# A block-convolution and token-mixer kernel: a second fold of the kv transform, Nyquist rows on column tiles, and a rewritten instruction order

## The chip, the core and the metric

The kernel runs on one core of a Trainium2 chip. The core has five engines with separate instruction streams: TensorE (PE; its weight loads are listed as PEld), VectorE (DVE), ScalarE (ACT), GpSimd (POOL) and SyncE (SP, which issues DMAs only; so can POOL). Each engine takes its instructions strictly in the order of its stream and waits on semaphores for the others. The metric is the device time of one execution in microseconds (us).

## What is computed

Two branches share the input x = A_q and are mixed by a gate. With S = 2048, D = 640, F = 1536:

```python
k_shift = sum over t of 4:  k_pad[:, t:t+S, :] * shift_k[:, 3 - t]
kv  = k_shift * v
kv_f = rfft(kv padded to 4096);  kf_f = rfft(ssm_k padded to 4096)
y   = irfft(kv_f * kf_f)[:S] + kv * ssm_D
a   = q * y
h   = layernorm(q)                       # over D
b   = (gelu(h^T @ w1 + b1) @ w2 + b2)^T  # mixes the tokens
g   = sigmoid((q * gate_w).sum(-1))
out = g * a + (1 - g) * b
```

## The kernel before

**The convolution.** The 2048 positions are cut into P = 4 blocks of n = 512. Filter block i (`W0` to `W3`) and kv block j (`A0` to `A3`) are taken to the frequencies of a length of 1024 by matmuls with cosine and sine tables (`TFc`, `TFs` for the filter, `AFc`, `AFs` for kv, `TI` for the way back). The frequencies stand in four groups `fi` of 128: groups 0 and 1 hold the odd ones, 2 and 3 the even ones. Before its transform a block is folded: its second half is added to and subtracted from the first half in reverse order, so that a matmul contracts 256 positions (two sub-blocks of 128) instead of 512. For the filter the folded tile is `en`, which is then transposed to `eo`; for kv it is `es`. Output block m sums over j <= m the products of `A_j` with the combined filter `W_{m-j}`; the sums are collected in `Z0`/`Z1`, and the way back (`inverse`) and `epilogue` turn `Z` into two halves `pb`, `qb` and these into rows of the output.

Per kv block (`kv_load`, `kv_block`, `a_freq`): a DMA transpose loads k as `kT`; 80 small matmuls with diagonal weights `dg` make the shifted k; ScalarE evicts it to `ks`; two DMA transposes bring it to `kn`; VectorE multiplies it by `vn` in place and folds it to `es`. `kT`, `vn` and `es` have two buffers each, `kn` and `ks` one. In `a_freq` each of 8 results (4 groups, cosine and sine) takes two sub-blocks times two halves of D, four 128x320 matmuls, and one eviction to `A`.

The **Nyquist row** (frequency 512, an alternating sum) of each filter block rides in row 0 of a sine result: in `w_freq`, four matmuls with one column of weights (`nyq`) are put between the sine matmuls of group 3, and `w_nyq` moves row 0 of `W[:, 8]` to `W[0, 4]` by one DMA of 1.2 KB behind a 160 KB copy within `W`, and clears the old row.

**The token mixer.** `bn_stats` and a scale on VectorE give `h`; 384 matmuls `h,w` with w1 (in six sets of two buffers' worth, three buffers `w1_0` to `w1_2`) give `gT`; 384 matmuls `gT,w` with w2 (buffers `w2_0`, `w2_1`) give the tiles `o1_0` to `o1_7`, each evicted with the gate factor 1 - g. Most of `o` is written out by SP, and the convolution's part is added to it in DRAM by accumulating DMAs that POOL issues (`acc0`, `acc1`); for the last block half of it is added on VectorE and written once. The gate g, the same rows reversed (`ggr`), is made by a matmul with a flip matrix from three bf16 pieces `gs`, split off on POOL in five steps (`gs`, `gd`).

**The order.** Nothing is scheduled on the chip: every operation of the program is recorded with a number, and the tuple `ORDER` lists all of them in the order in which they are emitted, found offline by a search over a cost model. Each engine's stream, and so each queue of DMAs, follows from it. A wait is emitted in the stream of the engine that issues the operation, so on SP and POOL it holds back every later DMA of that queue. PSUM has four slots of two banks, handed out in this order.

Helpers record each kind of work in one line, which is the one that the profile names: L307 matmuls, L641 `tensor_tensor`, L648/L649 `tensor_scalar`, L656 copies, L659 memsets, L683 activations, L275 plain DMAs, L262 DMA transposes, L268 indirect loads, L266/L270 accumulating stores, L864/L866 the layernorm statistics. Instructions are therefore told apart by their tiles.

Of the kernel before, what the change touches and what calls it, by code (L numbers as in the profile page):

```python
# [8 lines left out]
BF16 = mybir.dt.bfloat16  # L9
F32 = mybir.dt.float32  # L10
I32 = mybir.dt.int32
ACT = mybir.ActivationFunctionType
# [5 lines left out]
class _Tracker:  # L18
# [34 lines left out]
    def regions(self, ap):  # L53
# [4 lines left out]
        if info[0] == "DR":  # L58
            lo = hi = ap.offset
            for st, ct in ap.ap:  # L60
                lo += min(0, st * (ct - 1))
                hi += max(0, st * (ct - 1))
            return [("DR", 0, 1, lo // info[1], hi // info[1] + 1)]
# [42 lines left out]
        else:  # L106
# [10 lines left out]
            res.append((space, p0, p1, base + lo * esize, base + hi * esize))  # L117
        return res
# [197 lines left out]
def bass_gated_mix__ssm_conv_h3__mixer_token_mlp__prompt_kernel(  # L316
# [42 lines left out]
)  # L359


# [891 lines left out]
```

## Time and profile before

| | us |
|---|---|
| three runs | 203.32, 207.01, 214.42 |
| their median | 207.01 |
| the profiled execution | 202.34 |
| its span, first to last instruction | 200.5 |
| TensorE busy | 183.1 |
| VectorE busy | 179.8 |
| ScalarE busy | 119.5 |
| GpSimd busy | 89.4 |

The profile is of one execution. Its page gives the busy time of each engine, the same in 40 slices of the span, the chain of work that ended last, and groups of equal instructions with their mean duration, the idle time of the engine just before them and what ended it. Further views list the instructions of one engine in order of time (start, length, what, and the idle time before), the busy time of all engines in chosen stretches, and the DMAs with the time from issue to landing. Lengths of neighbours on TensorE and VectorE overlap a little, since they are pipelined, so the cost of one of many is the distance between starts.

### The profile page before, as it was taken

The numbers are of one execution on the slowest core, as the hardware profiler recorded it, in microseconds if no ns is written. First come the engines' busy times: TensorE is split into PE (matmuls) and PEld (weight loads), VectorE is DVE, ScalarE is ACT, GpSimd is POOL, SyncE is SP. The second block draws the span as 40 slices with busy tenths as digits, with TensorE's granted clock in tenths as the row PEclk, the third lists the DMA queues.
The fourth block names the chain that finished last, engine by engine and source line by source line (L and its number), as shares of the span: only waits on it lengthen the run. The fifth ranks groups of instructions, "written<-read, shape, count | busy, mean of one in ns | idle before, by whom it ended". The sixth has DMA issues, their size and how long they took to land.

```text
span 200.5 us, 3786 instructions
## 1 busy us (share of the span) xinstructions
PE 183.1 (91%) x1528; PEld 123.2 (61%) x1528; DVE 179.8 (90%) x227; ACT 119.5 (60%) x187; POOL 89.4 (45%) x110
## 2 busy tenths in 40 slices
PE   0599799999999999999999999849999999999991
PEld 0445363467567777667777776526776677777670
DVE  4378999788799999999999999989999799999865
ACT  5777787888995895634701478334363814551571
POOL 4320256741803564005329133963881548517560
PEclk9999999999999999999999999978999999999999
DMA  5999989999789999999659102032779868898895
GB/s 143 237 234 283 254 230 207 248 254 281 216 189 204 181 131 158 179 288 221 201 157 210 29 0 65 0 109 85 217 150 280 238 152 263 171 201 252 174 148 113
DMA packets 49731, 36.86 MB, mean 184 GB/s; under 512 B 33202, under 2 KB 46386, under 8 KB 49714
## 3 DMA queue, kind: packets, MB, share of 16 engines
q1 hardware_dynamic: 43874, 20.17, 47.6%
q0 software_dynamic: 5840, 16.45, 33.3%
q8 instruction: 12, 0.20, 0.4%
q14 instruction: 5, 0.04, 0.1%
HBM read 23.25 MB, written 4.92 MB: 140 GB/s over the span
## 4 chain that ended last, share of the span: by engine, by line
PE 50%; DMA 12%; DVE 11%; SPq 11%; POOL 9%; issue 5%; ACT 0%; DVEq 0%; POOLq 0%
PE pp L307 50%; SPq L262 7%; DVE stats L864 4%; POOL out_dram L266 4%; DMA w<-in_B_w_dram 4%; SPq L275 3%; DMA wnat<-in_A_ssm_k_dram 3%; DMA out_dram<-cg 3%; POOL gd L641 2%; DVE en L641 2%; DVE cg L641 1%; DMA out_dram<-o 1%; DMA vn<-in_A_v_dram 1%; POOL gs L656 1%; POOL xe L268 1%
## 5 line engine op out<-in xcount | busy, mean ns | idle before, releaser
L307 PE MATMUL pp<-h,w 128*128 128x320 bf16 x384 | 54.3, 299 | 0.1
L307 PE MATMUL pp<-gT,w 128*128 128x320 bf16 x384 | 53.8, 301 | 0.5 <-DMA w<-in_B_w_dram 0.5
L641 DVE TENSOR_TENSOR tT<-A,W 128x640 bf16<-128x640 bf16 (+4 forms) x44 | 48.5, 1124 | 0.7
L641 DVE TENSOR_TENSOR Z<-Z,tT 128x2560 bf16<-128x2560 bf16 (+3 forms) x35 | 47.6, 1373 | 0.6
L307 PEld LDWEIGHTS pp<-gT,w 128*128 128x128 bf16 x384 | 37.6, 99 | 15.9 <-DMA w<-in_B_w_dram 0.8
L307 PEld LDWEIGHTS pp<-h,w 128*128 128x128 bf16 x384 | 37.2, 98 | 15.3 <-issue 1.0
L275 POOL DMA_DIRECT2D w<-in_B_w_dram x18 | 18.4, 1023 | 37.2 <-PE pp L307 34.0
L683 ACT ACTIVATE o<-pp,c,omg 128x640 bf16<-128x640 f32 x16 | 14.1, 880 | 20.4 <-PE pp L307 20.4
L683 ACT ACTIVATE A<-pp 128x640 bf16<-128x640 f32 x32 | 21.3, 707 | 6.2 <-PE pp L307 6.1
L683 ACT ACTIVATE gT<-pp,bf 128x640 bf16<-128x640 f32 x12 | 9.6, 797 | 18.9 <-PE pp L307 18.9
L307 PE MATMUL pp<-Z,TI 128*128 128x320 bf16 x128 | 20.1, 310 | 0.0
L268 POOL DMA_INDIRECT xe<-in_A_q_dram,bidx x8 | 11.4, 1427 | 14.2 <-PE pp L307 7.7
L266 POOL DMA_INDIRECT out_dram<-cg,bidx x8 | 15.9, 1984 | 4.2 <-issue 1.8
L683 ACT ACTIVATE W<-pp 128x640 bf16<-128x640 f32 x24 | 15.5, 711 | 3.2 <-PE pp L307 3.0
L307 PEld LDWEIGHTS pp<-Z,TI 128*128 128x128 bf16 x128 | 12.5, 100 | 5.7 <-issue 0.4
L864 DVE BATCH_NORM_STATS2 stats<-xs 128x6 f32<-128x320 bf16 x32 | 13.8, 475 | 1.4 <-DMA xs<-in_A_q_dram 1.4
L307 PE MATMUL pp<-eo,TFs 128*128 128x320 bf16 x64 | 12.8, 323 | 1.3 <-DMA eo<-en 1.0
L683 ACT ACTIVATE ks<-pp 128x1024 bf16<-128x1024 f32 (+1 forms) x12 | 10.2, 878 | 4.2 <-PE pp L307 3.4
L307 PE MATMUL pp<-eo,TFc 128*128 128x320 bf16 x64 | 12.4, 306 | 0.0
L268 POOL DMA_INDIRECT vn<-in_A_v_dram,bidx x8 | 11.1, 1386 | 2.1 <-issue 2.1
L683 ACT ACTIVATE xs<-xs 128x640 bf16<-128x640 bf16 x16 | 11.8, 747 | 0.0
L641 DVE TENSOR_TENSOR Z<-A,W 128x5120 bf16<-128x5120 bf16 x4 | 11.3, 2817 | 0.0
(85 smaller groups left out, 227.1 us busy)
## 6 DMA issues: line engine op xcount, KB each, us to landing
w<-in_B_w_dram POOLq DMA_DIRECT2D x8, 768.0 KB, 7.3
w<-in_B_w_dram POOLq DMA_DIRECT2D x10, 512.0 KB, 5.3
wnat<-in_A_ssm_k_dram SPq DMA_DIRECT2D x4, 640.0 KB, 5.7
xs<-in_A_q_dram SPq DMA_DIRECT2D x7, 320.0 KB, 3.7
out_dram<-o SPq DMA_DIRECT2D x6, 320.0 KB, 3.6
vn<-in_A_v_dram SPq DMA_DIRECT2D x4, 320.0 KB, 7.7
xe<-in_A_q_dram SPq DMA_DIRECT2D x4, 320.0 KB, 4.4
w<-in_B_w_dram SPq DMA_DIRECT2D x4, 256.0 KB, 5.2
```

Of the source, the lines that this page charges most:

```text
L262: ins = engobj.dma_start_transpose(out_ap, in_ap)
L266: ins = engobj.indirect_dma_start(whole, off, in_ap, None, compute_op=ALU.add)
L268: ins = engobj.indirect_dma_start(out_ap, None, whole, off)
L275: ins = engobj.dma_start(out_ap, in_ap)
L307: ins = self.nc.tensor.matmul(ps_ap, lhsT=lhsT, rhs=rhs, start=start, stop=stop)
L641: return vop(eng, c, lambda e: e.tensor_tensor(out_, in0, in1, op), [in0, in1], [out_], pr)
L656: return vop(eng, c, lambda e: e.tensor_copy(out_, in_), [in_], [out_], pr)
L683: return e.activation(out_, src, func, **kw)
L864: vop("DVE", 0.41, (lambda o_, i_: lambda e: e.bn_stats(o_, i_))(o_, i_), [i_], [o_], pr)
```

## The change

1. **kv's even frequencies are folded a second time.** The sub-blocks of a kv block are now taken 256 apart (`rows2`, strides of 256 rows; tables at 512 half steps), so that the two folded sub-blocks differ, at an even frequency, only by a sign. Two VectorE instructions per block add and subtract them into a new tile `fs` (one buffer), and each even group needs one sub-block instead of two. The epilogue takes its rows in the same new grouping.
2. **Nyquist rows on four column tiles.** `nyq` becomes 32 columns wide; eight matmuls of 32 columns by 160 (two sub-blocks, four tiles) and four with a one-row operand come after the sine matmuls of group 3, and write to a part of the same PSUM bank; ScalarE evicts them to `nr`, VectorE adds neighbouring blocks' `nr`, and four small DMAs per block, instead of one, bring them to `W[0, 4]`.
3. **Gate pieces**: the five steps of `gs`/`gd` move from POOL to VectorE.
4. **w1**: the eight later loads move from POOL's queue to SP's.
5. The first filter block is loaded and folded in two parts; `cg` has four buffers instead of two, used in turn, and the accumulating stores have two semaphores each; the last block adds `o1_6` and `o1_7`'s first rows on VectorE and stores the others early.
6. `ORDER` is new throughout. The tracker of dependencies holds output rows and PSUM banks apart differently.

```diff
-        iota(b["hcol_i"][:, :], [[256, 2]], 1, 2, 0.2)
+        iota(b["hcol_i"][:, :], [[512, 2]], 1, 2, 0.2)
...
-                        f"{nm}_{t0}" if s_ < 1 else f"{nm}_p", pr + 0.35 * (8 * hf + t0), stream="SP" if s_ < 1 else "POOL")
+                        f"{nm}_{t0}" if s_ < 1 else f"{nm}_p", pr + 0.35 * (8 * hf + t0), stream="SP")
...
-                    if c == 1 and fi == 3:
-                        pairs = pairs[:1] + [(b["nyq"][:, nb:nb + 1], eo[:, 0, nb, :]) for nb in range(2)] + pairs[1:]
-                    pe([p_], halves(p_, pairs), pr)
+                    mms = halves(p_, pairs)
+                    if c == 1 and fi == 3:
+                        for nb in range(2):
+                            for g in range(4):
+                                mms.append((p_, 320, 160, b["nyq"][:, nb, :], eo[:, 0, nb, 160 * g:160 * g + 160], nb == 0, False,
+                                            32 * g))
+                        for g in range(4):
+                            mms.append((p_, 320, 160, b["onr"][:, 0:32], eo[0:1, 1, 0, 160 * g:160 * g + 160], False, True, 32 * g))
+                    pe([p_], mms, pr)
...
+                    if c == 1 and fi == 3:
+                        act(b[f"nr{i}"][:, :], (lambda p_: lambda: pp[p_.slot][:, 320:480])(p_), ACT.Copy, 1, scale=1.0 / N2, ps=[p_])
...
+            tt(b[f"nr{i}"][:, :], b[f"nr{i}"][:, :], b[f"nr{i - 1}"][:, :], ALU.add, pr)
...
-            dma(W[0:1, 4, :], W[0:1, 8, :], f"wn{i}", 17)
-            memset(W[0:1, 8, :], 0.0, 2)
+            for g in range(4):
+                dma(W[0:1, 4, 160 * g:160 * g + 160], b[f"nr{i}"][32 * g:32 * g + 1, :], f"wn{i}", 17)
...
-            dma(b[nm][:, 0, :, :], rows(A_v, 2 * i), nm, pr + 0.3)
+            dma(b[nm][:, 0, :, :], rows2(A_v, 4 * i), nm, pr + 0.3)
...
+            e2 = es_[:, :, :].rearrange("p (e k) d -> p e k d", k=2)
+            for s_, op in ((0, ALU.add), (1, ALU.subtract)):
+                tt(b[f"fs{i % NFS}"][:, s_, :, :], e2[:, :, 0, :], e2[:, :, 1, :], op, pr - 2)
...
-                    e0 = 0 if (fi >= 2) == (c == 0) else 2
-                    pairs = [(tf(tab, nb, fi), es_[:, e0 + nb, :]) for nb in range(2)]
+                    if fi >= 2:
+                        pairs = [(tf(tab, 0, fi), b[f"fs{j % NFS}"][:, 3 - fi, c, :])]
+                    else:
+                        pairs = [(tf(tab, nb, fi), es_[:, 2 - 2 * c + nb, :]) for nb in range(2)]
...
-            cgs = [b[f"cg{k}"] for k in range(2)]
+            cgs = [b[f"cg{2 * (m_ % 2) + k}"] for k in range(2)]
...
-        copy(gs[:, 0, :], gg, 20, "POOL")
-        tt(gd[:, 0, :], gg, gs[:, 0, :], ALU.subtract, 20, eng="POOL")
-        copy(gs[:, 1, :], gd[:, 0, :], 20, "POOL")
-        tt(gd[:, 1, :], gd[:, 0, :], gs[:, 1, :], ALU.subtract, 20, eng="POOL")
-        copy(gs[:, 2, :], gd[:, 1, :], 20, "POOL")
+        copy(gs[:, 0, :], gg, 20, "DVE")
+        tt(gd[:, 0, :], gg, gs[:, 0, :], ALU.subtract, 20)
+        copy(gs[:, 1, :], gd[:, 0, :], 20, "DVE")
+        tt(gd[:, 1, :], gd[:, 0, :], gs[:, 1, :], ALU.subtract, 20)
+        copy(gs[:, 2, :], gd[:, 1, :], 20, "DVE")
```

What the new order does around these edits, read off the two programs: before the first `kn` multiplication VectorE now has all eight gate multiplications (`xs,gwb`) and three of the six instructions that combine neighbouring filter blocks, where it had six and one. On SP, the load of the first `kT` moves from the eighth place to behind the second filter transpose. Between the transposes that bring in the second `kn` and the load of the third `kT`, SP has 28 DMAs where it had 8: three of the w1 loads, four copies within `W`, the 16 small DMAs of the Nyquist rows, two table transposes, one load of v, and those transposes themselves. The flip matmul of the gate comes behind 120 of the 384 `gT,w` matmuls, before behind 24. After the last `Z` TensorE has 24 `gT,w` matmuls left, before 48.

More of the change, by code (lines that the diff above doesn't have):

```diff
@@ L58, in regions @@
         if info[0] == "DR":
[L59 to L63, printed above, removed]
+            parts = [(st, ct) for st, ct in ap.ap if st > info[1]]
+            offs = [ap.offset]
+            for st, ct in parts:
+                offs = [o + st * k for o in offs for k in range(ct)]
+            ext = sum(st * (ct - 1) for st, ct in ap.ap if st <= info[1])
+            return [("DR", 0, 1, o // info[1], (o + ext) // info[1] + 1) for o in offs]
         space, base, rowsize, esize = info
@@ L117, in regions @@
             res.append((space, p0, p1, base + lo * esize, base + hi * esize))
+        if space == "PS":
+            res = [(space, p0, p1, lo // 2048 * 2048, -(-hi // 2048) * 2048) for space, p0, p1, lo, hi in res]
         return res
@@ L544, in _build @@
         buf("idp", [128, 128], BF16, 0, 34)
-        buf("nyq", [128, 2], BF16, 0, 40)
+        buf("nyq", [128, 2, 32], BF16, 0, 40)
+        for i in range(P):
+            buf(f"nr{i}", [128, 160], BF16, 8, 50)
         buf("onr", [1, 256], BF16, 0, 40)
@@ L581, in _build @@
             buf(f"es{i}", [128, NB, D], BF16, 48, 90)
-        buf("tT", [128, 8, D], BF16, 42, END)
+        NFS = 1
+        for i in range(NFS):
+            buf(f"fs{i}", [128, 2, 2, D], BF16, 48, 90)
+        buf("tT", [128, 8, D], BF16, 50, END)
         for j in range(P):
@@ L788, in _build @@
         for nb in range(2):
-            ts(b["nyq"][:, nb:nb + 1], b["par_i"][:, :], -2.0, 1.0, ALU.mult, ALU.add, 0.6, eng="DVE")
+            ts(b["nyq"][:, nb, :], bc(b["par_i"][:, :], [[1, 128], [0, 32]]), -2.0, 1.0, ALU.mult, ALU.add, 0.6, eng="DVE")
             memset(TFs[:, nb * 512:nb * 512 + 1], 0.0, 0.6)
-        memset(b["nyq"][0:1, 0:1], 0.5, 0.6)
+        memset(b["nyq"][0:1, 0, :], 0.5, 0.6)
         memset(TFc[0:1, 0:512], 0.5, 0.6)
-        memset(TFs[0:1, 0:1], 1.0, 0.6)
         memset(TFs[0:1, 256:384], -1.0, 0.6)
@@ L901, in w_turn @@
             eo = b[f"eo{i % 2}"]
[L902 to L905 removed]
+            for c0, c1 in W_PARTS[i]:
+                fw = wn[:, c0:c1, 256:512].rearrange("p c (k u) -> p k c u", k=2)
+                bw = bass.AP(tensor=wn, offset=256 + c0 * n, ap=[[DC * n, 128], [-128, 2], [n, c1 - c0], [-1, 128]])
+                for e, op in ((0, ALU.add), (1, ALU.subtract)):
+                    tt(en[:, 2 * e:2 * e + 2, c0 * 128:c1 * 128].rearrange("p k (c u) -> p k c u", c=c1 - c0), fw, bw, op,
+                       1.0 + 0.1 * i)
             x0 = en[:, 2, :].rearrange("p (c u) -> p c u", c=DC)[:, :, 0:1]
@@ L916, in w_turn @@
                 for k in range(2):
-                    p_ = _PS()
-                    pe([p_], [(p_, c * 128, 128, en[:, 2 * e + k, c * 128:(c + 1) * 128], ident, True, True)
-                              for c in range(DC)], 1.0 + 0.1 * i)
+                    p_ = _PS(True)
+                    for c0, c1 in W_PARTS[i]:
+                        pe([p_], [(p_, c * 128, 128, en[:, 2 * e + k, c * 128:(c + 1) * 128], ident, True, True)
+                                  for c in range(c0, c1)], 1.0 + 0.1 * i)
                     act(eo[:, e, k, :], flat(p_), ACT.Copy, 0.3, ps=[p_])
@@ L1104, in mlp2 @@
                 dma(rows(out, q), b[f"o1_{q}"][:, :, :], f"o1_{q}", 1.5)
-            elif q == NO - 1:
-                for k in range(2):
-                    dma(rows1(out, 2 * q + k), b[f"o1_{q}"][:, k, :], f"o1_{q}_{k}", 1.5)
+            else:
+                dma(rows1(out, 2 * q + 1), b[f"o1_{q}"][:, 1, :], f"o1_{q}", 1.5)
         def tabs(c, fi, i):
@@ L1162, in epilogue @@
                             if k:
-                                t_ = 4 * m_ + 3 - i
-                                dma(rows1(out, t_), c_, f"acc1_{i}", 1.0, stream="POOL", accum=True, idx=back(t_), whole=whole(out))
-                            else:
-                                tt(c_, c_, b[f"o1_{q}"][:, i, :], ALU.add, pr)
-                                dma(rows1(out, 2 * q + i), c_, "last", 1.0)
+                                t_ = 4 * m_ + 3 - 2 * i
+                                dma(rows1(out, t_), c_, f"acc1_{i}_{m_ % 2}", 1.0, stream="POOL", accum=True, idx=back(t_), whole=whole(out))
+                            else:
+                                tt(c_, c_, b[f"o1_{q + i}"][:, 0, :], ALU.add, pr)
+                                dma(rows1(out, 4 * m_ + 2 * i), c_, "last", 1.0)
             if last:
@@ L1175, in epilogue @@
                 if k == 0:
-                    dma(rows(out, q), cg, "acc0", 1.0, stream="POOL", accum=True)
+                    dma(rows2(out, 4 * m_), cg, f"acc0_{m_ % 2}", 1.0, stream="POOL", accum=True)
                     continue
                 for i in range(2):
-                    t_ = 4 * m_ + 3 - i
-                    dma(rows1(out, t_), cg[:, i, :], f"acc1_{i}", 1.0, stream="POOL", accum=True, idx=back(t_), whole=whole(out))
+                    t_ = 4 * m_ + 3 - 2 * i
+                    dma(rows1(out, t_), cg[:, i, :], f"acc1_{i}_{m_ % 2}", 1.0, stream="POOL", accum=True, idx=back(t_), whole=whole(out))
         def finish(m_):
@@ L1220, in _build @@
         plan.run(ORDER)
-        for nm in ("acc0", "acc1_0", "acc1_1", "last"):
+        for nm in sorted(k for k in T.dma_sems if k.startswith("acc") or k == "last"):
             T.wait_dma_final("SP", nm)
```

36 lines of the change are left out of this document (19 added, 17 removed), and 65 rows, old and new, of the table ORDER.

## The prediction

> **What bounds the kernel now.** The page's busy times come first, then VectorE's and the DMA engines' slices, then the shares of the chain of work that ended last.
>
> ```profile
> PE 183.1 (91%) x1528; PEld 123.2 (61%) x1528; DVE 179.8 (90%) x227; ACT 119.5 (60%) x187; POOL 89.4 (45%) x110
> ...
> DVE  4378999788799999999999999989999799999865
> ...
> DMA  5999989999789999999659102032779868898895
> ...
> PE 50%; DMA 12%; DVE 11%; SPq 11%; POOL 9%; issue 5%; ACT 0%; DVEq 0%; POOLq 0%
> ```
>
> Two engines are nearly full, and the chain names TensorE. But a chain picks one of two engines that are both busy; which one holds the end is seen by stretches. I cut the span at the first `kn` multiplication (51.5) and at the end of the last `Z` (187.5). The columns are the stretch, its length, the busy time of PE, PEld, DVE, ACT and POOL, the granted clock, the DMA engines' share and GB/s.
>
> ```profile
> 0.00:51.50 51.50, 42.69 (x380) 24.32 (x381) 39.28 (x99) 39.57 (x63) 19.78 (x56) 1.00 1.01 237
> 51.50:187.50 136.00, 131.44 (x1087) 92.71 (x1085) 132.56 (x115) 73.85 (x117) 65.12 (x52) 0.99 0.75 169
> 187.50:200.50 13.00, 8.96 (x66) 6.20 (x64) 7.99 (x15) 6.04 (x8) 4.50 (x3) 1.00 0.75 130
> ```
>
> In the middle stretch VectorE is idle for 136.00 - 132.56 = 3.44 us, TensorE for 4.56. VectorE's instructions in order of time show how little of that is a wait, and give the prices used below.
>
> ```profile
> 51.52 1.49 DVE L641 TENSOR_TENSOR kn<-kn,vn 128x2560 bf16<-128x2560 bf16 x1 [2.24 <-issue]
> 53.05 1.56 DVE L641 TENSOR_TENSOR es<-kn 128x1280 bf16<-128x1280 bf16 x2
> 54.52 2.89 DVE L641 TENSOR_TENSOR W<-W,W 128x2560 bf16<-128x2560 bf16 x2
> 57.33 0.82 DVE L641 TENSOR_TENSOR xs<-xs,gwb 128x1280 bf16<-128x1280 bf16 x1
> 58.06 4.29 DVE L641 TENSOR_TENSOR W<-W,W 128x2560 bf16<-128x2560 bf16 x3
> ...
> 96.57 1.48 DVE L641 TENSOR_TENSOR kn<-kn,vn 128x2560 bf16<-128x2560 bf16 x1
> ...
> 135.26 0.82 DVE L641 TENSOR_TENSOR cg<-cg,xe 128x1280 bf16<-128x1280 bf16 x1 [0.76 <-ACT xe L683]
> ...
> 157.52 0.82 DVE L641 TENSOR_TENSOR cg<-cg,xe 128x1280 bf16<-128x1280 bf16 x1 [1.32 <-ACT xe L683]
> ...
> 186.66 0.88 DVE L641 TENSOR_TENSOR Z<-Z,tT 128x640 bf16<-128x640 bf16 x2
> ...
> 189.98 0.82 DVE L1154 CAST pb<-pp 128x640 bf16<-128x640 f32 x1 [0.84 <-PE pp L307]
> ...
> 195.42 0.49 DVE L641 TENSOR_TENSOR cg<-pb,qb 128x640 bf16<-128x640 bf16 x1 [1.64 <-DMA out_dram<-cg]
> ```
>
> In the middle only two waits are marked, 0.76 and 1.32; the other 1.36 are small gaps between instructions that depend on each other. So VectorE runs through from 51.52 to 187.46 on work alone, and the span is three terms: the time of the first `kn` (51.5), VectorE's work from there to the last `Z` (136), and a tail of 13.0. TensorE is nearly as full, but is not what holds this chain. In the front all 16 DMA engines are busy (share 1.01), and VectorE idles 51.50 - 39.28 = 12.2.
>
> **The change, part by part.** TensorE first.
>
> ```profile
> 17.07 1.51 PE L307 MATMUL pp<-kT,dg 64*64 64x256 bf16 x48
> 18.52 0.31 PE L307 MATMUL pp<-eo,TFs 128*128 128x320 bf16 x1
> ...
> 20.11 1.07 PE L307 MATMUL pp<-kT,dg 64*64 64x256 bf16 x32
> ...
> 59.19 6.68 PE L307 MATMUL pp<-h,w 128*128 128x320 bf16 x48
> 65.71 2.34 PE L307 MATMUL pp<-es,AFc 128*128 128x320 bf16 x16
> ...
> 82.10 1.07 PE L307 MATMUL pp<-kT,dg 64*64 64x256 bf16 x32
> ...
> 133.12 0.25 PE L307 MATMUL pp<-gs,flip 128*128 128x16 bf16 x3 [3.54 <-POOL gs L656]
> ```
>
> A 128x320 matmul costs (65.71 - 59.19) / 48 = 0.136. The second fold removes eight per kv block, 32 in all: 4.35 us, all in the middle. The Nyquist row: from 18.52 to 20.11 stand four sine matmuls and four of one column, 1.59 in all; less 4 x 0.136 the four cost 1.05, or 0.26 each, 4.2 for the four blocks. The twelve that replace them have no row. The nearest is the tiled `kT` matmul, 48 in 1.45, 0.030 each: 0.36 per block, a gain of 2.8 in all. The far bound is twelve at 0.26: 3.1 per block, a loss of 8.3. I take the near row, since these too are tiles with distinct partitions of the result. That gain is in the front, in front of the evictions. The 3.54 for `gs` goes too, since the flip matmul now stands behind 120 `gT,w` matmuls (16 us) instead of 24. All of this is TensorE's time, and I cost it at nothing: VectorE covers it. If that cover were gone it would be worth 4.35 + 3.54 = 7.9.
>
> VectorE gains work. A 128x1280 instruction takes 58.06 - 57.33 = 0.73 from start to start, so the eight `fs` cost 5.9. Five gate pieces, three additions of `nr` and the split of the first fold have no row of their size; the nearest small one and the large one that is split are these.
>
> ```profile
> L641 DVE TENSOR_TENSOR en<-wnat 128x1280 bf16<-128x1280 bf16 x8 | 6.7, 847 | 4.6 <-DMA wnat<-in_A_ssm_k_dram 4.6
> ...
> L866 DVE BATCH_NORM_AGGREGATE mv<-stats 128x2 f32<-128x12 f32 x16 | 3.0, 198 | 0.2
> ```
>
> At 0.2 each the gate pieces cost 1.0, nearer than the upper bound of 0.73 each, as they hold 16 elements; the three `nr` and the split cost 0.8 in the front. The new order also draws two gate multiplications (1.46) and two combinations of filter blocks (57.33 - 54.52 = 2.81) from behind the first `kn` to ahead of it. VectorE's middle term is 132.56 + 5.84 + 1.0 - 1.46 - 2.81 = 135.1, with the small gaps of 1.36 some 136.4: as before without its two waits. The second fold is paid for by what moved to the front.
>
> The front then holds 39.28 + 1.46 + 2.81 + 0.8 = 44.4 of VectorE's work. Were its idle 12.2 kept, the first `kn` would come at 56.6. But 2.24 of it is the wait at that `kn`, which moved work now fills, and 4.6 is waiting for filter loads, ahead of which the new order has five `bn_stats`; the first `kT`, a slow transpose, no longer stands ahead of the tiles on SP. On the other side the third combination needs the last filter block, which in the new order comes behind two `kT`-shaped loads. I take 5 of idle: first `kn` at 49.5, between 47 and 52.
>
> Tail: with four `cg` buffers the wait of 1.64 on an accumulating store goes, and with 24 matmuls instead of 48 behind the last `Z` (3.3 less) TensorE's part of it should no longer hold VectorE for 0.84. 13.0 - 1.64 - 0.84 is 10.5. POOL's last two accumulating stores then are late next, at about that time.
>
> The waits that it adds are on SP. These are SP's issues between the second `kn` and the third `kT`, and times from issue to landing.
>
> ```profile
> 54.68 1.56 SPq L262 DMA_TRANSPOSE kn<-ks  x1
> 56.28 1.27 SPq L275 DMA_DIRECT2D W<-W  x2
> 57.60 2.39 SPq L262 DMA_TRANSPOSE kn<-ks  x1
> ...
> 65.50 0.55 SPq L275 DMA_DIRECT2D W<-W  x1
> 66.10 14.85 SPq L262 DMA_TRANSPOSE kT<-in_A_k_dram  x2
> ...
> 87.27 3.67 SPq L262 DMA_TRANSPOSE kn<-ks  x2
> ```
>
> ```profile
> w<-in_B_w_dram POOLq DMA_DIRECT2D x10, 512.0 KB, 5.3
> ...
> W<-W SPq DMA_DIRECT2D x4, 160.0 KB, 6.1
> ...
> kn<-ks SPq DMA_TRANSPOSE x8, 5.3
> ...
> kT<-in_A_k_dram SPq DMA_TRANSPOSE x4, 11.2
> ```
>
> The third `kT` was issued at 66.10, 14.6 after the first `kn` and 11.4 after the second block's `kn` transposes; 8 DMAs lay between, now 28. Twenty more at 0.57 (57.60 - 56.28, halved, is 0.66; 66.10 - 65.50 is 0.60, with gaps) are 11.4 to 12: issue at 26 after the first `kn`, and the first Nyquist piece waits for its copy's landing (6.1) within that. It lands 11.2 later, at 37; 5.2 more to the third `kn` transposes (before, from 82.10 to 87.27, by the same steps); but SP has the fourth `kT` ahead of them (26 + 14.85 and three issues, 43), then two transposes of 1.84, landing 5.3 after issue: 50. VectorE reaches the third `kn` in the old order at 96.57 - 51.52 = 45.1, in the new one, with four `fs` more (2.9), 4.3 of work moved ahead, and products over 7680 elements drawn forward (1.43 per 2560 by the row at 58.06, 4.3), at 48. So it waits about 2 there, between 0 and 5. The fourth I cost at 0.5. The cleared rows and w1 issues that leave POOL gain nothing; four more evictions on ScalarE lie beside its idle (60% busy).
>
> Sum: 49.5 + 136.4 + 10.5 + 2.5 = 198.9; with the 202.34 - 200.5 = 1.84 around the span, 200.7 as a profiled execution, 0.8% below 202.34. The median of the runs, 207.01, is 1.023 times the profiled one: 205.
>
> **Rivals.** *The front shrinks in earnest.* The front is bound by DMA, and what stands ahead of the first `kn` has changed: half the first w1 set comes behind its operands. If it comes at 47 and the third `kn` is in time, the span is 47 + 136.4 + 10.5 = 193.9, the time 195.7 x 1.023 = 200. For: 12.2 of idle, share 1.01. Against: the third combination waits for the last filter block, behind slow transposes.
>
> *TensorE was the bound.* Then 4.35 and 3.54 come off and VectorE's 6.8 is hidden: 202.34 - 7.9 = 194.4, times 1.023 is 199. For: the chain gives it 50%. Against: 3.44 of VectorE's idle in 136.
>
> *SP is late (slower).* One queue now carries w1, transposes and row copies. If the third `kT` is issued at over 31 after the first `kn` instead of 26 (the fourth then follows at its pace), the third `kn` keeps VectorE for 5 more, and the w1 sets queued behind these two keep TensorE, whose `ks` of the fourth block come behind w1 matmuls: as much again there, 10 in all. 198.9 + 10 + 1.84 = 210.7, times 1.023 is 215.6. For: 28 DMAs, and `kT` landing 11.2 after issue where w1 takes 5.3. Against: before, SP waited at times in this stretch (57.60 to 66.10 holds more than its issues).
>
> The Trainium skill ("DMA: Bandwidth & Descriptors", section on queues, rings and completion order) speaks for this rival: each DMA engine takes turns between queue rows, but works off one row's ring in order. By that rule a w1 load on POOL's queue took turns with `kT`, and on SP's stands behind it. The rows agree so far as that w1 landed in 5.3 while `kT` took 11.2; no run here yet shows w1 behind `kT`.
>
> *The Nyquist tiles run one after the other* at 0.26: 8.3 more on TensorE in the front, some of it hidden by evictions; the last filter block comes later by up to that, 207 x 1.023 = 212.
>
> **Chances.** Two per cent is about what a measurement of this kernel can tell from no change: 202.9 and 211.1 around 207.01, which is 2.2 below and 5.9 above the forecast. The forecast's case gets 0.42 (within 2% 0.33, faster 0.05, slower 0.04), its own range 201 to 211. The shorter front gets 0.28 (0.25 faster, 0.03 same), TensorE as bound 0.07, SP late 0.20 (0.18 slower, 0.02 same), the Nyquist tiles 0.03. Faster 0.37, same 0.38, slower 0.25. The range leaves out the far end of SP's delays and a front under 47: 197.5 to 212.
>
> **What would show it.** The first `kn` near 49.5; VectorE without marked waits from there but for one at the third `kn`; TensorE with several us of idle time between, as its saving comes out as waiting; the twelve Nyquist matmuls within 0.5 per block; the third `kT` 26 after the first `kn`; no wait on an accumulating store in the tail. It is wrong if TensorE stays full to the end, if `kn` waits add up to over 6, or if the runs scatter other than before's, which my factor of 1.023 assumes.

## The result, and the profile after

The changed kernel takes 202.45 us (median of 19 executions, 199.34 to 205.22); the kernel before, run 16 more times beside it, has a median of 203.32 over all 19. The ratio is 0.988, 95% interval 0.985 to 0.992: 1.2% faster. Medians here are over all executions, ratios leave out the disturbed ones, so the two can differ. The forecast of 205 lies above both medians: as a time it was on the wrong side of the kernel before, though its range, 197.5 to 212, holds the result.

Of the profile page of the changed kernel (202.12 us, span 200.3), the busy times, the slices of PE, DVE and the granted clock, and the shares of the chain:

```profile
PE 177.9 (89%) x1528; PEld 120.3 (60%) x1528; DVE 182.7 (91%) x245; ACT 121.5 (61%) x192; POOL 78.8 (39%) x90
...
PE   0189989999999998999999699999999949999990
...
DVE  5799988998999999999997599999999999689873
...
PEclk9999999999999999999999999999999996999999
...
PE 27%; DVE 25%; DMA 24%; SPq 9%; issue 5%; ACT 4%; POOL 4%; DVEq 0%
```

TensorE has 5.2 us less work, VectorE 2.9 more, and the chain is no longer TensorE's: it hops between TensorE, VectorE and DMAs, a quarter each. The same three stretches as before, cut at the first `kn` and the last `Z` (columns as in the prediction):

```profile
0.00:48.31 48.31, 37.66 (x385) 22.07 (x386) 42.20 (x108) 39.12 (x62) 26.66 (x55) 1.00 1.00 233
48.31:187.26 138.95, 132.41 (x1089) 92.83 (x1088) 132.62 (x125) 76.29 (x123) 44.38 (x31) 0.99 0.68 171
187.26:200.30 13.04, 7.82 (x58) 5.39 (x56) 7.85 (x14) 6.04 (x8) 7.73 (x5) 0.99 0.74 138
```

The front gained 3.2, the middle gave 2.9 of it back, and the tail is as long as it was. VectorE in order of time shows the middle's two long waits (a third, at 178.47, is 0.53) and the tail's three, and in the tail two neighbours on which a later section rests:

```profile
95.08 1.48 DVE L650 TENSOR_TENSOR kn<-kn,vn 128x2560 bf16<-128x2560 bf16 x1
...
112.44 1.49 DVE L650 TENSOR_TENSOR kn<-kn,vn 128x2560 bf16<-128x2560 bf16 x1 [3.53 <-issue]
...
173.44 0.82 DVE L650 TENSOR_TENSOR cg<-cg,xe 128x1280 bf16<-128x1280 bf16 x1 [1.89 <-ACT xe L692]
...
187.18 0.81 DVE L650 TENSOR_TENSOR cg<-pb,qb 128x1280 bf16<-128x1280 bf16 x1
188.02 0.82 DVE L650 TENSOR_TENSOR cg<-cg,xe 128x1280 bf16<-128x1280 bf16 x1
189.68 0.82 DVE L1186 CAST pb<-pp 128x640 bf16<-128x640 f32 x1 [0.84 <-PE pp L310]
...
191.86 0.82 DVE L1186 CAST pb<-pp 128x640 bf16<-128x640 f32 x1 [0.29 <-PE pp L310]
...
193.29 0.49 DVE L650 TENSOR_TENSOR cg<-pb,qb 128x640 bf16<-128x640 bf16 x1 [0.61 <-ACT qb L692]
```

The third `kn` doesn't wait, the fourth does. What leads up to it, on SP's queue and GpSimd's (two views of the same kernel; GpSimd's second line is a gather of the tail), and the median times from issue to landing:

```profile
73.89 4.45 SPq L265 DMA_TRANSPOSE kT<-in_A_k_dram  x1
...
87.10 3.10 SPq L265 DMA_TRANSPOSE kn<-ks  x2
...
101.25 5.80 SPq L265 DMA_TRANSPOSE kn<-ks  x2
107.11 0.57 SPq L278 DMA_DIRECT2D w<-in_B_w_dram  x1
```

```profile
100.79 2.21 POOL L278 DMA_DIRECT2D w<-in_B_w_dram  x2 [13.99 <-PE pp L310]
...
184.60 4.26 POOL L271 DMA_INDIRECT xe<-in_A_q_dram,bidx  x1 [0.31 <-issue]
```

```profile
w<-in_B_w_dram SPq DMA_DIRECT2D x10, 512.0 KB, 4.9
...
kn<-ks SPq DMA_TRANSPOSE x8, 4.7
kT<-in_A_k_dram SPq DMA_TRANSPOSE x4, 6.4
```

The third `kT` is issued at 73.89, 25.6 after the first `kn` (forecast 26), but it lands in 6.39 where it took 14.28 (6.4 and 11.2 are medians of all four `kT` loads). The fourth block's `kn` transposes are issued half a microsecond behind two w2 loads of 768 KB each, and take 5.80 of SP's time where the third block's took 3.10. TensorE's own longer waits are for weights and for a table (0.82 at 78.23, 1.78 at 113.72, 0.61 at 155.53, 2.75 at 164.97).

### The profile page after: what moved, and what is told of

The parts are those of the page before. It is cut to its first block, busy times and chain, and to the rows that moved or that the text cites. A ratio compares the mean times of both kernels' runs of the same rounds, so it can differ in the third digit from the quotient of the medians.

```text
span 200.3 us, 3798 instructions
## 1 busy us (share of the span) xinstructions
PE 177.9 (89%) x1528; PEld 120.3 (60%) x1528; DVE 182.7 (91%) x245; ACT 121.5 (61%) x192; POOL 78.8 (39%) x90
## 4 chain that ended last, share of the span: by engine, by line
PE 27%; DVE 25%; DMA 24%; SPq 9%; issue 5%; ACT 4%; POOL 4%; DVEq 0%
PE pp L310 27%; SPq L278 8%; DVE tT L650 7%; DVE Z L650 6%; DMA kn<-ks 5%; DMA w<-in_B_w_dram 4%; DMA xe<-in_A_q_dram,bidx 4%; DVE cg L650 3%; DMA eo<-en 3%; DMA xs<-in_A_q_dram 3%; DMA TI<-AFs 3%; DVE stats L880 2%; POOL xe L271 2%; DMA W<-W 2%; ACT ks L692 2%
## 5 line engine op out<-in xcount | busy, mean ns | idle before, releaser
L310 PE MATMUL pp<-gT,w 128*128 128x320 bf16 x384 | 55.3, 305 | 3.4 <-DMA w<-in_B_w_dram 3.4
L310 PE MATMUL pp<-h,w 128*128 128x320 bf16 x384 | 55.0, 299 | 2.1 <-DMA w<-in_B_w_dram 1.8
L650 DVE TENSOR_TENSOR tT<-A,W 128x640 bf16<-128x640 bf16 (+4 forms) x44 | 48.0, 1119 | 0.1
L650 DVE TENSOR_TENSOR Z<-Z,tT 128x2560 bf16<-128x2560 bf16 (+3 forms) x35 | 47.0, 1367 | 0.1
L278 POOL DMA_DIRECT2D w<-in_B_w_dram x8 | 9.6, 1204 | 59.0 <-PE pp L310 59.0
L271 POOL DMA_INDIRECT vn<-in_A_v_dram,bidx x8 | 16.4, 2044 | 14.0 <-DVE kn L650 12.5
L310 PE MATMUL pp<-Z,TI 128*128 128x320 bf16 x128 | 18.7, 300 | 0.8 <-DMA TI<-AFs 0.8
L692 ACT ACTIVATE ks<-pp 128x1024 bf16<-128x1024 f32 (+1 forms) x12 | 10.2, 880 | 11.2 <-PE pp L310 6.0
L271 POOL DMA_INDIRECT xe<-in_A_q_dram,bidx x8 | 14.7, 1836 | 4.4 <-DVE cg L650 2.9
L310 PE MATMUL pp<-eo,TFc 128*128 128x320 bf16 x64 | 13.2, 320 | 0.3 <-DMA eo<-en 0.3
L310 PE MATMUL pp<-eo,TFs 128*128 128x320 bf16 x64 | 11.3, 311 | 0.8 <-ACT eo L692 0.5
```

Source lines behind the costliest of these rows:

```text
L271: ins = engobj.indirect_dma_start(out_ap, None, whole, off)
L278: ins = engobj.dma_start(out_ap, in_ap)
L310: ins = self.nc.tensor.matmul(ps_ap, lhsT=lhsT, rhs=rhs, start=start, stop=stop)
L650: return vop(eng, c, lambda e: e.tensor_tensor(out_, in0, in1, op), [in0, in1], [out_], pr)
L692: return e.activation(out_, src, func, **kw)
```

## The experiments

All edits are to the changed kernel. Runs of one group shared a chip and the runs of the kernel before; groups are compared by their ratio to it.

**First group: which engine, and SP.**

> The changed kernel once more, as the measure for the runs beside it, and to test the factor of 1.023. My forecast was 200.7 as a profiled execution and 205 by that factor. If the median of three runs of the kernel before (207.01) was an accident of scattered runs, its median here is near its profiled execution (202.3), and the changed kernel stands at 0.985 to 0.995 of it, 200 to 202. If the factor was a property of this kernel, both medians are 2% above their profiled executions, near 207 and 205.

Median 202.90, ratio 0.991 (0.985 to 0.997); the kernel before 203.33 over 29 runs, and 205.81, 204.45, 205.01 and 204.88 beside the later groups. So the medians of the kernel before lie 0.5 to 1.7% above its profiled execution (202.34), those of the changed kernel 0.1 to 0.8% above theirs. The factor of 1.023 was that of three scattered runs.

`fs` for three blocks nearly left out:

```diff
-                tt(b[f"fs{i % NFS}"][:, s_, :, :], e2[:, :, 0, :], e2[:, :, 1, :], op, pr - 2)
+                w_ = D if i == 0 else 32
+                tt(b[f"fs{i % NFS}"][:, s_, :, 0:w_], e2[:, :, 0, 0:w_], e2[:, :, 1, 0:w_], op, pr - 2)
```

> Leaves out nearly all of the second fold's sums for the kv blocks 1 to 3 (32 of 640 columns are summed), so six instructions of VectorE shrink from 0.73 us to about 0.1, 3.8 us in all, and nothing moves. If VectorE is what holds the stretch from the first kn to the last Z, the time falls by 2.5 to 3.8. If TensorE holds it (its waits are for weights and for the inverse table, none of them for VectorE), the time stays within 0.7.

`fs` read by two matmuls instead of one:

```diff
-                        pairs = [(tf(tab, 0, fi), b[f"fs{j % NFS}"][:, 3 - fi, c, :])]
+                        pairs = [(tf(tab, 0, fi), b[f"fs{j % NFS}"][:, 3 - fi, c, :])] * 2
```

> Each of the 32 matmuls on the twice folded operand is run twice (accumulated, so that the even frequencies come out doubled): 32 x 0.136 = 4.35 us more on TensorE, the work that the second fold removed, with VectorE's work unchanged. If VectorE holds the middle stretch, TensorE's idle time there (6.5 us) takes it: at most 1.2 longer. If TensorE holds it, 3.5 to 4.4 longer.

Medians 200.56 (ratio 0.990, 0.984 to 0.996) and 204.16 (1.001, 0.995 to 1.007). The first is 2.3 us below the changed kernel by the medians, but its ratio is not to be told from 0.991, so this run alone does not decide. The ratio of the second is 1.0% above 0.991, 2 us; its median is 1.3 above. The middle stretch of the changed kernel's second profile, of the one with less on VectorE and of the one with more on TensorE, one line from each:

```profile
50.52:187.76 137.24, 130.15 (x1084) 91.91 (x1084) 132.63 (x125) 76.29 (x123) 43.54 (x31) 1.00 0.68 174
```

```profile
50.36:185.34 134.98, 129.82 (x1082) 91.80 (x1083) 128.84 (x125) 76.26 (x123) 49.25 (x31) 1.00 0.70 176
```

```profile
49.78:188.43 138.65, 134.21 (x1115) 95.12 (x1116) 132.76 (x125) 76.26 (x123) 41.19 (x31) 1.00 0.67 172
```

3.79 less on VectorE shortened the stretch by 2.26, 4.06 more on TensorE lengthened it by 1.41. These are single profiles, and the changed kernel's own stretch is 138.95 and 136.84 in its two others, so differences of this size are not clear of the scatter. Neither theory's number came out. Part of what VectorE saved became waiting: the fourth `kn` waited 3.98 instead of the 3.97 of the second profile although two blocks' sums ahead of it were gone, and a `Z` product waited 0.88 for a Nyquist piece.

The w1 loads back on GpSimd's queue:

```diff
-                        f"{nm}_{t0}" if s_ < 1 else f"{nm}_p", pr + 0.35 * (8 * hf + t0), stream="SP")
+                        f"{nm}_{t0}" if s_ < 1 else f"{nm}_p", pr + 0.35 * (8 * hf + t0), stream="SP" if s_ < 1 else "POOL")
```

> The eight later w1 loads go back to GpSimd's queue; SP keeps the transposes and the row copies. By the rival in which SP is late, w1 stands behind slow transposes: the fourth kn's wait of 3.53 and TensorE's wait of 1.78 for w1 go, 2 to 4 us shorter. By my reading the fourth kn waits because TensorE reaches the last kT matmuls late (99.08) and the transposes of ks run beside weight loads: the wait stays, only TensorE's 1.78 goes, and the time stays within 0.8; earlier w1 loads may then slow the transposes of kT (landing 6.4 now, 11.2 in the kernel before, where w1 was on GpSimd's queue), which would cost up to 2.

Median 204.81, ratio 1.004 (0.999 to 1.009): 1.3% slower than the changed kernel, so without this one part nothing is left of the gain. TensorE's row for the third block's `kT`, and the landing times, from its profile (that execution took 208.83, the longest of the 13, so the wait is that of a long one):

```profile
92.03 1.92 PE L310 MATMUL pp<-kT,dg 64*64 64x256 bf16 x32 [7.18 <-DMA kT<-in_A_k_dram]
```

```profile
w<-in_B_w_dram POOLq DMA_DIRECT2D x10, 512.0 KB, 5.5
...
kT<-in_A_k_dram SPq DMA_TRANSPOSE x4, 10.3
```

The rival in which SP is late had the sign wrong. With w1 on another queue the `kT` transposes land in 10.3 instead of 6.4 and TensorE waits 7.18 for one; with w1 behind them on SP they land first. The third one alone lands in 14.13 here, in 14.28 in the kernel before, which had w1 on GpSimd's queue too, and in 6.39 in the changed kernel. The Trainium skill's rule on queues and rings ("DMA: Bandwidth & Descriptors", section on queues, rings and completion order), that a DMA engine takes turns between queues but works off one queue's ring in order, agrees with these numbers. I had read it only for its harm to w1. The medians of w1 hardly differ (5.5 and 4.9), but the two w1 loads issued beside the third and fourth `kT` landed in 11.59 and 11.22 here, in 12.71 and 10.59 in the kernel before, and in 4.64 and 4.31 in the changed kernel: both sides of the shared turns were paying.

**Second group: the waits for w2, and the `cg` buffers.** Two inverse matmul groups (16 matmuls, the third output block's first half) go ahead of the `gT,w` matmuls that wait for w2, an eviction that frees their PSUM with them:

```diff
-    539, 612, 607, 610, 585, 541, 542, 678, 586, 587, 493, 679, 606, 8, 621, 644, 609, 588, 645, 655,
+    539, 493, 612, 607, 610, 585, 541, 644, 645, 542, 678, 586, 587, 679, 606, 8, 621, 609, 588, 655,
```

> The 16 inverse matmuls of the third output block's first half stand ahead of the gT,w matmuls that wait 2.75 for a w2 load at 164.97 (1.94 in the second profile of the changed kernel), so TensorE works through the load's landing. If TensorE holds the middle stretch, 2 to 2.75 shorter. If VectorE holds it, 0 to 0.8 (only the tail's wait of 0.84 for TensorE can go). If both share it, as the two runs before suggest (3.6 less of VectorE gave 2.25, 4.35 more of TensorE cost 1.4), about 1.

The first two w2 loads issued by SP:

```diff
-            dma(b[nm][:, :, :], dram(B_w2, q * 256, [[S, 128], [128 * S, FT], [1, 256]]), nm, 40.0 + q,
-                stream="POOL")
+            dma(b[nm][:, :, :], dram(B_w2, q * 256, [[S, 128], [128 * S, FT], [1, 256]]), nm + ("s" if q < 2 else ""), 40.0 + q,
+                stream="SP" if q < 2 else "POOL")
```

> The first two w2 loads (768 KB each) are issued by SP behind the fourth block's kn transposes and the last w1 load, not by GpSimd beside them. If those two loads are what stretches the transposes (5.80 on SP, landing 9.31, against 3.1 and about 5 for the third block's), the fourth kn comes 3 to 4 earlier, VectorE's wait there (3.53 and 3.97 in two profiles) falls under 1, TensorE's wait for w1 at 113.72 goes too, and the time is 1.5 to 3.5 shorter. If the three w1 loads ahead of them are the cause, the wait stays above 2.5 and the time within 0.7.

Two `cg` buffers again:

```diff
-            cgs = [b[f"cg{2 * (m_ % 2) + k}"] for k in range(2)]
+            cgs = [b[f"cg{k}"] for k in range(2)]
```

This kernel also puts each operation that would then come too early behind what it needs.

> Two cg buffers instead of four, the order otherwise as it is. My prediction gave the two more buffers 1.64, the tail's wait on an accumulating store. If that holds, the wait is back and the time 1 to 2 longer; one store in the middle may cost up to 1 more. If another tail wait (TensorE's last inverse matmuls, ScalarE's qb) ends as late, within 0.5.

> Both moves together: the inverse matmuls ahead of the wait for w2, and the first two w2 loads behind the kn transposes. If the two waits hit two engines that share the bound, together 3 to 5 shorter than the changed kernel, 198 to 200; if VectorE alone holds, as the second move alone; if neither, within 0.7.

The w2 loads on SP: 200.06, ratio 0.985 (0.978 to 0.992); repeated in a later group 198.68, 0.982 (0.977 to 0.987). Its SP queue, its fourth `kn` and its landing time:

```profile
102.42 2.79 SPq L265 DMA_TRANSPOSE kn<-ks  x2
105.27 3.70 SPq L278 DMA_DIRECT2D w<-in_B_w_dram  x3
```

```profile
109.64 1.48 DVE L650 TENSOR_TENSOR kn<-kn,vn 128x2560 bf16<-128x2560 bf16 x1
```

```profile
kn<-ks SPq DMA_TRANSPOSE x8, 3.6
```

The transposes take 2.79 again, the wait of 3.53 is gone, TensorE's 1.78 too. The two w2 loads were the cause, not the w1 loads ahead of them, which are still there.

The inverse matmuls forward were predicted to gain or to do nothing; the kernel is slower than the one before: 206.00, ratio 1.017 (1.011 to 1.023). Its middle stretch is no longer than the changed kernel's (136.72, by its first `kn` at 48.77 and last `Z` at 185.49), its tail is 16.91. Both moves together: 202.94, with executions from 197.83 to 205.82. With two `cg` buffers 218.79, ratio 1.081 (1.075 to 1.086): VectorE then waits 7.52 and 3.89 for accumulating stores. Here three VectorE instructions had to change places in the order, so the size is not that of the buffers alone; that the new order can't do with two of them is.

**Third group: what happened in the tail.** GpSimd's row in the kernel with the inverse matmuls forward, and VectorE's rows at that time:

```profile
179.01 8.14 POOL L271 DMA_INDIRECT xe<-in_A_q_dram,bidx  x1 [2.08 <-DVE cg L618]
```

```profile
185.42 0.81 DVE L618 TENSOR_TENSOR cg<-pb,qb 128x1280 bf16<-128x1280 bf16 x1
186.27 0.83 DVE L618 TENSOR_TENSOR cg<-cg,xe 128x1280 bf16<-128x1280 bf16 x1
187.09 0.82 DVE L1154 CAST pb<-pp 128x640 bf16<-128x640 f32 x1
190.64 0.53 DVE L618 TENSOR_TENSOR cg<-pb,qb 128x640 bf16<-128x640 bf16 x1 [2.73 <-ACT qb L660]
```

The same gather took 1.04 in the changed kernel's first profile. It ended at 187.15, near the end of VectorE's run of products of two operands in SBUF. In the kernel with both moves an accumulating store was held, to 184.84, and VectorE's run ended there too:

```profile
175.23 9.61 POOL L269 DMA_INDIRECT out_dram<-cg,bidx  x1 [0.30 <-issue]
```

```profile
182.50 0.81 DVE L618 TENSOR_TENSOR cg<-pb,qb 128x1280 bf16<-128x1280 bf16 x1
183.34 0.83 DVE L618 TENSOR_TENSOR cg<-cg,xe 128x1280 bf16<-128x1280 bf16 x1
184.84 0.82 DVE L1154 CAST pb<-pp 128x640 bf16<-128x640 f32 x1 [0.67 <-PE pp L310]
```

In the first of the two kernels ScalarE, in order, stood behind the gather with its `qb`, and VectorE and TensorE behind that. A VectorE copy of one column that has to wait for ScalarE tests it (operation 743; three operations move up so that the wait is real):

```diff
+        copy(b["gs"][:, 0, 0:1], b["o1_6"][:, 0, 0:1], 20, "DVE")
...
-    695, 703, 551, 696, 706, 556, 697, 653, 549, 690,
+    695, 551, 653, 549, 743, 703, 696, 706, 556, 697, 690,
```

> The kernel with the inverse matmuls moved forward, and in addition one VectorE copy of a single column in its last run of Z instructions, which has to wait for a ScalarE result and so makes VectorE pause for about 0.5 to 1.1 us near 182. In that kernel GpSimd's gather of xe, issued at 179.01, took 8.14 and ended at 187.15, as VectorE's unbroken run of Z instructions ended (187.09), and the tail then waited for it. If VectorE's unbroken run is what holds GpSimd's descriptors up, the gather now ends at the pause (before 184), and the time is 1.5 to 3 shorter than that kernel's 206.0 although VectorE waits. If the gather is slow for another reason (the DMA engines, its own data), the pause only costs: 0.5 to 1 longer.

202.62, ratio 0.993 (0.989 to 0.998), against 1.017 without the copy: 2.4% less, relative to the kernel before, by making VectorE wait (no run has the three moved operations without the copy). VectorE and GpSimd of this kernel:

```profile
181.83 0.49 DVE L618 TENSOR_TENSOR tT<-A,W 128x640 bf16<-128x640 bf16 x1
183.35 0.16 DVE L633 COPY gs<-o 128x1 bf16<-128x1 bf16 x1 [1.03 <-ACT o L660]
```

```profile
175.87 7.99 POOL L269 DMA_INDIRECT out_dram<-cg,bidx  x1 [0.30 <-issue]
184.17 1.05 POOL L271 DMA_INDIRECT xe<-in_A_q_dram,bidx  x1 [0.30 <-DVE Z L618]
```

This time it is a store that was held, from 175.87 to 183.86, half a microsecond past the end of the pause (182.32 to 183.35), and the gather behind it took 1.05. So a break in VectorE's unbroken work lets GpSimd in. How long it has to be can be read from the traces. VectorE's next instruction mostly starts before the one ahead of it has ended; call it a break where it does not, however short. In the rows above, 182.50 and 0.81 make 183.31, and the next starts at 183.34: a break of 34 ns. In the 19 profiles of the changed kernel and its variants, each of the 17 gathers behind 130 that took over 3.4 ended 0.87 to 0.95 us behind the first break since its issue, and each of the six stores held in VectorE's last run ended 1.52 to 1.54 behind it. In two of these 23 (the copy in this kernel and in one below) the break was the pause; in the others it was of 34 or 35 ns, and no copy out of PSUM is needed for it. Five of the gathers were held in the middle of a run, with no pause and no such copy at their end, as this one in the kernel with the w2 loads on SP (the break is at 167.14):

```profile
162.84 5.25 POOL L271 DMA_INDIRECT xe<-in_A_q_dram,bidx  x1 [0.30 <-DVE tT L650]
```

```profile
164.26 2.88 DVE L650 TENSOR_TENSOR Z<-Z,tT 128x2560 bf16<-128x2560 bf16 x2
167.18 1.56 DVE L650 TENSOR_TENSOR tT<-A,W 128x1280 bf16<-128x1280 bf16 x2
```

A break is not the only way in: most indirect DMAs take 1.0 to 2.2 without one, sixteen stores issued between 155 and 167 took 3.0 to 3.5 with none, and a gather of v issued at 38 to 40 took 3.9 to 8.3 in thirteen profiles, in some with a break 0.82 before its end and in some with none. That so short a break, put in by an edit, would free GpSimd as the pause did was not tested.

The Trainium skill ("SBUF — State Buffer", section on who interferes with whom) states that a VectorE instruction with two inputs in SBUF contends with a GpSimd instruction that reads SBUF. The traces agree as far as that goes: the indirect DMAs, which take their row numbers from the SBUF tile `bidx`, were held beside runs of `TENSOR_TENSOR`, and none of GpSimd's plain DMAs behind 130 took over 1.96. The same section reports a probe in which `tensor_tensor` did not stall a DMA; here it did, and the measurement decides. That a hold of 8 to 10 us outlasts a dozen VectorE instructions and ends behind a break is in the traces alone.

The last block's gather then gets a buffer of its own and goes ahead of three stores:

```diff
+        buf("xl", [128, 2, D], BF16, 91, END)
...
-            xes = [b[f"xe{k}"] for k in range(2)]
+            xes = [b["xe0"], b["xl" if last else "xe1"]]
```

> The kernel with the first two w2 loads on SP, and a buffer of its own for the last output block's gather, whose two DMAs go ahead of three accumulating stores on GpSimd's queue. If the gather held up beside VectorE's run sets the tail, ScalarE's wait for it (1.53) and VectorE's of 0.74 go: 0.5 to 1 shorter than that kernel's 200.06. If TensorE's last 32 inverse matmuls set the tail, within 0.4.

> The same early gather, with both moves (inverse matmuls forward, first two w2 loads on SP), whose tail waited 5.45 for the gather. If that is why the two moves together gave nothing (202.94), the time is now 4 to 5 shorter, 197 to 199, below either move alone. If forwarding the inverse matmuls costs for another reason, it stays above 201.

> The changed kernel beside them, as the measure on the same chip: 0.985 to 0.995 of the kernel before.

200.73 (ratio 0.984, 0.976 to 0.993), a miss: now a store was held for 7.68, and GpSimd's last store, which sets the end, was issued at 192.76, later than without the edit (191.00). 204.58 with both moves, from 195.60 to 205.68: in its profile the gather, issued at 175.38, took 10.25. The place was still inside VectorE's run. The changed kernel beside them: 202.80.

**Fourth group: the gather out of VectorE's run.** It is issued with the first block's, near 138 (the same buffer, and one store a place forward), without the inverse matmuls forward, with them, and with the pause too.

> The first two w2 loads on SP, the last block's gather in a buffer of its own and issued with the first block's (near 138, where GpSimd's gathers took 1.0 to 2.3 in every profile), and the accumulating store that was held up moved one place forward. If GpSimd's descriptors beside VectorE's last run are what is left in the tail, 197 to 199.5, since ScalarE and VectorE no longer wait for it; if the last accumulating stores behind it set the end (they ended 192.8 to 194.3 in the two profiles with these loads on SP), no change from 200.

> The same with the inverse matmuls forward. If the gather held up beside VectorE's run was the whole cost of that move, 195 to 197.5, and no execution above 201 (the two kernels with both moves so far scattered from 195.6 to 205.8). If the stores that take its place on GpSimd's queue are held up as long, it scatters again, median 200 or more.

> The same, and VectorE's one-column copy that waits for ScalarE near 180. If the store that remains in GpSimd's queue beside VectorE's last run is held up, the pause frees it: at most 1 longer than the kernel without it where that one is undisturbed, and shorter where it is not (195.5 to 198). If nothing is held up there any more, 0.5 to 1 longer.

> The kernel with only the first two w2 loads on SP, as the measure on the same chip: 0.980 to 0.988 of the kernel before.

198.40 (ratio 0.981, 0.976 to 0.987), 198.88 (0.979, 0.970 to 0.988), 198.79 (0.980, 0.975 to 0.985) and 198.68 (0.982). Moving the inverse matmuls forward no longer costs anything, and the scatter is gone (196.75 to 199.82), so their loss was the gather; but they gain nothing either. GpSimd without and with the pause, one line from each:

```profile
175.25 8.73 POOL L269 DMA_INDIRECT out_dram<-cg,bidx  x1 [0.85 <-DVE cg L619]
```

```profile
177.80 3.98 POOL L269 DMA_INDIRECT out_dram<-cg,bidx  x1 [1.59 <-DVE cg L619]
```

With the pause the stretch behind the last `Z` is 11.77 long, the shortest of all profiles, against 14.56 without; the pause and a first `kn` at 51.05 (48.94 without) take it back. All four are about 2% faster than the kernel before and, by the ratios, 0.7 to 1.2% faster than the changed kernel, which was not run in this group; the smallest edit among them, the two w2 loads on SP, does as well as the rest.

**Fifth group: the two engines again, without the wait at the fourth `kn`.** In the kernel with w2 on SP the middle is full on VectorE:

```profile
49.25:182.30 133.05, 129.78 (x1084) 92.10 (x1084) 132.38 (x125) 76.24 (x123) 41.06 (x29) 1.00 0.71 181
```

> The second fold's sums of blocks 1 to 3 left out again but for 32 columns (3.8 us of VectorE), now on the kernel whose fourth kn doesn't wait: there VectorE was busy for 132.38 of the middle's 133.05 and TensorE for 129.78. If VectorE holds the whole middle, the time is 2.5 to 3.3 shorter than that kernel's 198.68, where TensorE then sets in; if TensorE holds it, within 0.7.

> The 32 doubled matmuls (4.35 us of TensorE) on the same kernel. If VectorE holds the middle, TensorE's 3.3 of idle time takes most of it: 1 to 2 longer. If TensorE holds it, 4 to 4.4 longer.

198.13 (ratio 0.974, 0.967 to 0.981) and 201.16 (0.987, 0.979 to 0.995), on a chip on which that kernel itself was not run. In medians, 3.8 less on VectorE gave 0.55 and 4.35 more on TensorE cost 2.5; in ratios 0.8% and 0.5%. Sparing VectorE didn't shorten the middle (133.70 in this profile): where it ran through before, it now waits, 0.98 for a Nyquist piece and longest for the eviction of a TensorE result:

```profile
120.22 2.82 DVE L650 TENSOR_TENSOR tT<-A,W 128x5120 bf16<-128x5120 bf16 x1 [1.77 <-ACT A L692]
```

The first run, by its median, is what was expected if TensorE holds the middle; the second, by its ratio, what was expected if VectorE does. So neither holds it alone: VectorE is full there, and what it is spared turns into waits for TensorE and the Nyquist pieces. Sparing VectorE alone gains little; sparing TensorE alone was not tried.

## Why the prediction missed, step by step

**The step that failed** is the last of the sum: "The median of the runs, 207.01, is 1.023 times the profiled one: 205." The prediction named this factor itself as a sign of being wrong. As a profiled execution the forecast was 200.7, 0.8% below 202.34; the runs show 1.2% (0.8 to 1.5). The factor put the forecast above the median of the kernel before, 203.32 over 19 runs, so that against this median the forecast gain reads as a loss. With the 1.005 that these 19 give (203.32 / 202.34), it would have been 201.7. That the ratio was near is in part luck, as the terms below show.

**First `kn`, 49.5**: right. 48.31 here; seventeen more profiles with the same front have 48.70 to 51.12.

**VectorE's middle, 135.1 of work**: 132.6. The price of `fs` was right (3.79 for six that shrink by 0.63 each), and the four instructions moved ahead were the ones named. What was mis-sized is what neighbours save. Counted in the two traces, in the stretch before 77 of VectorE's instructions started before the one ahead had ended, by 6.30 us in all, and 35 came behind a short break (1.35 in all, most between a product `tT` and a sum into `Z`); now 113 overlap, by 8.90, and 8 come behind a short break, 0.39. This 2.6 more of overlap is most of the 2.5, and the small gaps, kept at 1.36 in the forecast, gained 1.0. It has a price: VectorE's run before the last `Z` has no break left from 178.5 to 188.0, where before there were four from 181.8 to 185.9, and none of GpSimd's indirect DMAs was held there.

**TensorE's saving at nothing**: half right. The doubled matmuls cost 1.3 to 2 us of 4.35, so in this balance the cover is thinner than TensorE's 6.5 of idle time, which is waits for weights and not slack.

**SP**: the issue of the third `kT` was right to 0.4, its landing not: I took 11.2, the median of four, of which the third beside w1 took 14.28, and it is 6.39 ahead of w1. Hence no wait at the third `kn` instead of 2. At the fourth, 3.53 instead of 0.5, by two w2 loads which I had left on GpSimd's queue without asking what they would meet.

**Tail, 10.5**: 13.0, mis-sized by 2.5. The wait for a store went, as forecast, but TensorE reached the last inverse matmuls at 187.31, no earlier than the last `Z` (187.26), so its 0.84 stayed; and the gather was held for 4.26 (184.60 to 188.86), again to 0.87 behind the first break of VectorE's run (187.99), so that ScalarE's `qb` came late.

**Nyquist**: twelve matmuls in 0.43 per block (18.89 to 19.32), forecast 0.36; the gate pieces 0.17 to 0.18 each, forecast 0.2. TensorE's wait at the flip went from 3.54 to 0.30.

The sum of the span (198.9, measured 200.3) was near because errors cancelled: front 1.2, VectorE's work 2.5 and third `kn` 2 better; fourth `kn` 3, tail 2.5 and the 1.89 at 173.44 worse. The last is of this one profile: the two others of the changed kernel have no wait there, and middles of 137.24 and 136.84. It stands behind TensorE's wait of 2.75 and the slow matmuls after it, of which the last section tells.

## What to carry to other kernels

Take the level from many runs of the kernel before, or forecast the ratio; three scattered runs are no factor. When a load changes queues, price what it stops sharing turns with as well as what it now stands behind: here the third transpose gained 8 us, and the loads beside it gained too. When an order sets VectorE's instructions so that each overlaps the next, look at what GpSimd issues in that stretch; a gather that is needed soon belongs ahead of VectorE's unbroken run.

## What the runs showed of the hardware

GpSimd's indirect DMAs took 1.0 to 2.2 us as a rule. In 18 of the 19 profiles of the changed kernel and its variants one of them took 3.5 to 10.3 beside VectorE's last run of SBUF products, and ended 0.87 to 0.92 (a gather) or 1.52 to 1.54 (a store) behind the first break of that run, mostly one of 34 or 35 ns. In the kernel before none behind 180 took over 1.7. GpSimd's plain DMAs behind 130 took at most 1.96 in all of them.

TensorE's granted clock fell behind some of its waits. In the changed kernel's first profile the 24 matmuls behind the wait of 2.75 took 5.11, and the clock in that window is 0.66 (in steps of one microsecond 0.99, three times 0.50, 0.80); 24 of the same kind take 3.42.

```profile
164.97 5.11 PE L310 MATMUL pp<-gT,w 128*128 128x320 bf16 x24 [2.75 <-DMA w<-in_B_w_dram]
...
191.66 3.42 PE L310 MATMUL pp<-gT,w 128*128 128x320 bf16 x24
```

```profile
165.00:170.00 5.00, 5.00 (x25) 3.09 (x26) 4.96 (x6) 0.83 (x1) 4.39 (x3) 0.66 1.07 274
```

Behind waits of 1.94 and 2.04 in the two other profiles of this kernel they took 3.43. A wait of 2.95 in the kernel with doubled matmuls was followed by matmuls at full pace, so length alone does not decide; nothing here settles what does.
